# Attention 14 places earlier, output weights split under the gated unit, first down weights split when their pool opens

## The chip, the cores and the metric

The kernel runs on one core of one Trainium2 chip. The metric is the device time of one execution in microseconds (us); of several runs the median is given. TensorE is called PE in the profile, VectorE DVE, ScalarE ACT, GpSimd POOL and SyncE SP; PEld is TensorE's loading of weights.

## The reference

A layer norm of `x` (2048 tokens by 448), then two branches that are added to `x`: attention with a compressive memory, and a gated linear unit.

```python
xn = _layernorm(x)
# attention: 16 heads of 28, 4 segments of L = 512 tokens, one after the other
logits = einsum("bhqd,bhkd->bhqk", qs, ks) * scale + mask     # causal within the segment
a_dot = einsum("bhqk,bhkd->bhqd", softmax(logits), vs)
a_mem = (phi(qs) @ M) / (phi(qs) @ z + 1e-6)                  # phi(t) = t + 1 if t > 0 else exp(t)
o = g * a_mem + (1 - g) * a_dot                               # g = sigmoid(beta), per head
M, z = M + phi(ks).T @ vs, z + sum(phi(ks))
attn = concat(o) @ wo
# gated unit, F = 1792
glu = (sigmoid(xn @ w_gate) * (xn @ w_up)) @ w_down
out = x + attn + glu
```

## The kernel before

All products are done in float32r with operands split in two, a high part and the residue (`split`: ScalarE copies the high part, VectorE subtracts), and three products per pair of operands; a product over 448 is 11 matmuls of up to 512 columns (`TERMS`).

The program has three parts. The *front* (L236 to L471) normalises and transposes `x` block by block (4 blocks of 512 tokens), computes values (`values`, `pv`), keys and queries (`keys_queries`, `pp`), the memory (`update`) and its recall (`recall`, `n2`), and stores queries and keys (`qd`), values (`vd`) and recalled parts (`md`) to DRAM. Then *attention* and the *gated unit* run interleaved, and last `project` multiplies the attention's output (`od` in DRAM, loaded to `ob`, transposed in `transpose_split` to `xs`) by the output weights `wo` (`po`, L668) and adds it to `acc`, which already holds `x` and receives the gated unit's products (`pd`, L154, added at L157); the result is stored from `acc`.

The gated unit is a generator (`gated`): 7 pairs of 128-wide slices of F, for each pair 4 token blocks, for each block two gate and two up products (`pgu`, L209, 11 matmuls each) and up to four down products of earlier blocks (`down`, 6 matmuls each). Each `yield` is a place. A dictionary `ahead` says at which places the next weights are loaded and split: the raw gate and up weights pass through one buffer (`raw`), the split ones through three buffers of 8 KB (`8k`), the down weights through two raw buffers and four split ones (`wdn`) in the pool `late`, which is opened when the front's pool is closed. The first 18 places stand in the front already, between its last products; the first down weights (slices 0 and 1) are split by the entry `ahead[1, 1]`, L193, right after those 18 places.

Attention is another generator (`attention`), of 234 steps: 16 units of four heads, 14 steps each (`SLOT`). A unit is two pairs of heads. A pair loads its queries and keys (`Pair.load`, L490, six DMAs into one of two `qk2` buffers), makes scores (`st`, L506), copies them (L509), masks them on GpSimd (L518), finds maxima on VectorE (L521, L536 to L549), subtracts (L557) and exponentiates (L558). `Unit.finish` multiplies by the values (`pa`, L583), transposes (`n1`, L590), normalises to `on` (L125) and stores to `od` from GpSimd's queue (L596).

The main loop runs the gated unit's places and then the projection's; after each it runs as many attention steps as keep attention evenly spread over the places from `LEAD` to the end less `TAIL`:

```python
k = NG * FILL + 6                                   # 18
for part in (ffn, project()):
    for _ in part:
        want = min(round(n_att * (k - LEAD) / (N_FFN + N_OUT - LEAD - TAIL)), n_att)
```

`N_FFN` is 548 and `N_OUT` 77, so that 234 steps fall on 625 - 32 - 55 = 538 places, 0.435 steps to a place. `project` opens with the load of `ob` and then loads, through the one `raw` buffer, the two halves of the output weights, each split when it is in (L645 to L652). The six downs that are left when the gated unit ends (`rest`) are run in its first places. `po` takes its bank by turns from the tag of the down products (`pd`, one bank) and from the scores' (`s`).

TensorE's order is the order of the program (`MANUAL`), in the front that of ScalarE and VectorE too (`FRONT`). Everything else is ordered by a scheduler, queue by queue, and each engine and each DMA queue then works in that order: SP's queue holds nearly all loads and stores.

Of the kernel before, what the change touches and what calls it, by code (L numbers as in the profile page):

```python
# [16 lines left out]
P = 128  # L17
# [17 lines left out]

LEAD, TAIL = 32, 55

# [19 lines left out]
def kernel(  # L57
# [86 lines left out]

    rest, late = [], []

    def gated():
# [26 lines left out]
        def ready_down(f):  # L174
            wdn[f] = late[0].tile([P, 2, D], F32R, name="wdn", bufs=4)
            split(wdn[f][:, 0, :], wdn[f][:, 1, :], raw_down[f])

        load_up(0)
        yield
# [8 lines left out]
        for f0 in range(0, NF, FG):  # L188

            ahead = {}  # L190
            if f0 == 0:
                ahead[0, 0] = lambda: ready_up(1)
                ahead[1, 1] = lambda: (ready_down(0), ready_down(1))  # L193
            if f0 + FG < NF:
# [4 lines left out]
                ahead[3, 2] = lambda: ready_up(f0 + 3)  # L199
                ahead[3, 3] = lambda: ready_down(f0 + 3)  # L200
            for b in range(NB):
                hs = []
# [33 lines left out]
    with tc.tile_pool(name="front", bufs=2) as sb, tc.manual_schedule(engines=FRONT):  # L236
# [100 lines left out]
        def recall(b, i, phi):  # L337
# [4 lines left out]
            weigh(sb, tb, n2, gate[:, HG * i:HG * (i + 1)], MEM_EPS)  # L342
            nc.sync.dma_start(md[b][:, :, GW * i:GW * (i + 1)], tb.rearrange("p (t j) d -> p t (j d)", t=NT))

# [129 lines left out]

    late.append(ctx.enter_context(tc.tile_pool(name="late", bufs=1, reuse_waits="tile")))
    sb = ctx.enter_context(tc.tile_pool(name="att", bufs=1, reuse_waits="tile"))

# [159 lines left out]
    def project():  # L637
# [3 lines left out]
        def load(b):  # L641
            nc.sync.dma_start(ob[b % 2][:, :, :D].bitcast(F32), od[b])
            nc.sync.dma_start(ob[b % 2][:, :, D:].bitcast(F32), od[b][:, :, 384:])

        load(0)  # L645
        raw = [mid.tile([P, 1024], F32, name="raw", bufs=1)[:, :2 * D] for _ in range(2)]
        wo = [eight_k(F32R, f"wo{n}").rearrange("p c n -> p (c n)")[:, :4 * D] for n in range(2)]
        wo3 = w_o.rearrange("p (h n) -> p h n", h=2)
        for h in range(2):
            nc.sync.dma_start(raw[h], wo3[:, h, :])  # L650
            part = slice(2 * D * h, 2 * D * (h + 1))
            split(wo[0][:, part], wo[1][:, part], raw[h])  # L652
        load(1)
        yield
        for n in range(NB * NT + 3):
# [8 lines left out]
            if n >= 3:  # L664
                b, t = divmod(n - 3, NT)
                po = bank("po", ("pd", "s", "s")[n % 3])
                for m, (a, w) in enumerate(TERMS):
                    T.matmul(po[:, :D], xs[b][:, a, t * P:(t + 1) * P], wo[w // 4][:, D * (w % 4):D * (w % 4 + 1)],  # L668
                             start=m == 0, stop=m == len(TERMS) - 1)
                    if m in (3, 7):  # L670
                        yield
# [56 lines left out]
```

## Time and profile before

| | |
|---|---|
| median of 3 runs | 729.49 us (728.47 to 730.18) |
| profiled execution | 728.81 us, of which the span 727.1 us |
| granted TensorE clock | 0.99 of full speed over the span |
| gated unit's products (L209) | 1232 matmuls, mean 398 ns |
| down products (L154) | 672 matmuls, mean 373 ns |
| scores (L506), weighted values (L583) | 256 and 512 matmuls |
| projection (L668) | 176 matmuls |

The profile shows one execution. Matmuls are pipelined, so a mean of 398 ns is the time in the pipe, and a group of 11 takes 2.55 us. A timeline row has start, length (both us), engine, line, operation, the tiles out<-in, shapes, the count, and in brackets how long the engine stood idle before it and what ended that. A row of waits has the total, the count and the longest. A row of groups has the count, busy time, mean ns, and idle time before.

### The profile page before, as it was taken

How to read it: one execution, taken by the hardware profiler on the slowest of the kernel's cores; microseconds unless marked ns; L12 is line 12 of the kernel's file. 1: busy time of each engine (PE TensorE's matmuls, PEld its weight loads, DVE VectorE, ACT ScalarE, POOL GpSimd, SP SyncE). 2: the span in 40 equal slices, each digit the busy share in tenths (PEclk: the TensorE clock that was granted, in tenths of full speed). 3: DMA queues.
4: the chain of work that ended last, by engine and by line, in shares of the span. 5: the costliest groups of instructions: out<-in, count | busy, mean ns of one | idle time of the engine just before them, and what ended most of it. 6: DMA issues, size and time to landing. Idle time of an engine off the chain costs nothing.

```text
span 727.1 us, 10861 instructions
## 1 busy us (share of the span) xinstructions
PE 708.5 (97%) x3788; PEld 587.2 (81%) x3788; DVE 560.9 (77%) x1030; ACT 338.2 (47%) x552; POOL 147.9 (20%) x349
## 2 busy tenths in 40 slices
PE   7999999999999999999999999999999999998898
PEld 6888888887887877878878777787787877876697
DVE  5676776455599888898888898898788898888653
ACT  3635444231355554565545555455454555444320
POOL 4310000000131212222223223242222332322100
PEclk7999999999999999999999999999999999999999
DMA  9443546675343223322333225232422233223242
GB/s 311 185 174 133 218 178 236 227 252 134 98 106 86 74 66 94 107 78 67 109 103 88 59 83 133 71 88 79 127 66 73 64 92 85 82 74 110 84 159 89
DMA packets 58278, 86.24 MB, mean 119 GB/s; under 512 B 20080, under 2 KB 36976, under 8 KB 57712
## 3 DMA queue, kind: packets, MB, share of 16 engines
q1 hardware_dynamic: 56944, 81.88, 36.2%
q0 software_dynamic: 1280, 3.67, 1.4%
q8 instruction: 30, 0.49, 0.3%
q14 instruction: 24, 0.20, 0.1%
HBM read 53.81 MB, written 31.72 MB: 118 GB/s over the span
## 4 chain that ended last, share of the span: by engine, by line
PE 62%; DVE 18%; issue 8%; POOL 6%; ACT 3%; DMA 3%; SPq 0%; POOLq 0%; ACTq 0%; DVEq 0%
PE pgu L209 22%; PE pd L154 10%; PE pp L295 8%; PE pv L284 6%; PE po L668 5%; DVE mx L521 4%; DVE w L557 4%; PE st L506 3%; PE pa L583 3%; POOL w L518 2%; DVE acc L157 2%; DVE mb L549 2%; PE n L341 1%; PE pmm L323 1%; POOL on L595 1%
## 5 line engine op out<-in xcount | busy, mean ns | idle before, releaser
L209 PE MATMUL pgu<-xs,wgu 128*128 128x512 f32 x1232 | 321.7, 398 | 0.0
L209 PEld LDWEIGHTS pgu<-xs,wgu 128*128 128x128 f32 x1232 | 225.7, 188 | 44.9 <-issue 1.8
L154 PE MATMUL pd<-wdn,hh 128*128 128x448 f32 x672 | 165.3, 373 | 7.2 <-DVE acc L157 3.6
L154 PEld LDWEIGHTS pd<-wdn,hh 128*128 128x128 f32 x672 | 123.3, 190 | 23.7 <-DVE acc L157 3.7
L518 POOL TENSOR_SCALAR_AFFINE_SELECT w<-w 128x256 f32<-128x256 f32 (+1 forms) x160 | 72.1, 451 | 332.8 <-ACT w L509 330.9
L558 ACT ACTIVATE w<-w 128x1024 f32<-128x1024 f32 (+1 forms) x96 | 86.8, 914 | 84.3 <-DVE w L557 81.6
L521 DVE TRANSPOSE_TENSOR_REDUCE mx<-w 128x32 f32<-128x1024 f32 (+1 forms) x96 | 101.1, 1056 | 23.3 <-POOL w L518 23.1
L509 ACT ACTIVATE w<-st 128x512 f32<-128x512 f32 x160 | 93.5, 588 | 53.0 <-PE st L506 52.9
L557 DVE TENSOR_TENSOR w<-w,mb 128x1024 f32<-128x1024 f32 (+3 forms) x128 | 108.6, 872 | 0.4
L295 PE MATMUL pp<-xs,wqk 128*128 128x512 f32 x308 | 77.3, 399 | 0.0
L157 DVE TENSOR_TENSOR acc<-pd,acc 128x448 f32<-128x448 f32 x112 | 67.7, 606 | 8.0 <-PE pd L154 7.9
L295 PEld LDWEIGHTS pp<-xs,wqk 128*128 128x128 f32 x308 | 56.6, 189 | 11.8
L506 PE MATMUL st<-qk 84*128 84x128 f32 (+3 forms) x256 | 63.9, 311 | 0.0
L506 PEld LDWEIGHTS st<-qk 84*128 84x128 f32 x256 | 48.3, 189 | 8.9 <-ACT w L509 0.4
L220 ACT ACTIVATE hh<-sg 128x512 fp32r<-128x512 f32 x56 | 35.1, 626 | 43.5 <-DVE sg L218 38.4
L549 DVE STREAM_TRANSPOSE mb<-top 128x1024 f32<-128x1024 f32 x32 | 39.7, 1241 | 13.0 <-POOL top L546 12.9
L217 ACT ACTIVATE sg<-pgu 128x512 f32<-128x512 f32 x56 | 33.3, 595 | 34.7 <-PE pgu L209 34.5
L284 PE MATMUL pv<-wv,xs 128*128 128x448 f32 x176 | 42.2, 396 | 3.2 <-ACT xs L98 3.2
L221 DVE SCALAR_TENSOR_TENSOR hh<-sg,hh 128x512 fp32r<-128x512 f32 x56 | 39.6, 706 | 6.5 <-ACT hh L220 6.3
L218 DVE SCALAR_TENSOR_TENSOR sg<-sg,pgu 128x512 f32<-128x512 f32 x56 | 37.4, 668 | 9.0 <-PE pgu L209 8.8
L301 DVE TENSOR_TENSOR qk<-pp,qk 128x512 fp32r<-128x512 f32 x28 | 19.3, 690 | 30.7 <-ACT e L300 23.6
L284 PEld LDWEIGHTS pv<-wv,xs 128*128 128x128 f32 x176 | 35.0, 205 | 7.4 <-ACT xs L98 4.1
(94 smaller groups left out, 626.3 us busy)
## 6 DMA issues: line engine op xcount, KB each, us to landing
qk<-qd SPq DMA_DIRECT2D x192, 112.0 KB
qd<-qk SPq DMA_DIRECT2D x28, 512.0 KB
raw<-in_w_ffn SPq DMA_DIRECT2D x14, 512.0 KB
vd<-vst SPq DMA_DIRECT2D x4, 1024.0 KB
vv<-vd SPq DMA_DIRECT2D x16, 256.0 KB
od<-on POOLq DMA_DIRECT2D x16, 224.0 KB, 3.7
ob<-od SPq DMA_DIRECT2D x4, 896.0 KB
out<-acc SPq DMA_DIRECT2D x16, 224.0 KB
```

The source lines that it names most:

```text
L154: T.matmul(pd[:, :D], l, r, start=n == 0, stop=n == len(mms) - 1)
L157: V.tensor_add(acc[b][:, t, :], pd[:, :D], acc[b][:, t, :])
L209: T.matmul(dst, wgu[f][:, w, side * P:(side + 1) * P], xs[b][:, a, :], start=n == 0, stop=n == len(TERMS) - 1)
L284: T.matmul(pv[:, :D], xs[b][:, a, t * P:(t + 1) * P], wv[:, w, :], start=n == 0, stop=n == len(TERMS) - 1)
L295: T.matmul(pp, wqk[c][:, w, :], xs[b][:, a, :], start=n == 0, stop=n == len(TERMS) - 1)
L506: T.matmul(st[:, at:at + L - kb * P], self.qk[:KS, 1, h, kb * P:(kb + 1) * P], self.qk[:KS, 0, h, kb * P:], start=True, stop=True)
L509: A.activation(w, st, AF.Copy)
L518: G.affine_select(d, d, pattern=pattern, base=0, channel_multiplier=-1, compare_op=ALU.is_ge, fill=MASK)
L521: V.tensor_reduce(mx[:, 16 * n0:16 * (n + 1)], self.w[:, n0 * L:(n + 1) * L].rearrange("p (b n) -> p b n", n=32), axis=mybir.AxisListType. ...
L549: V.transpose(mb.rearrange("p h (b n) -> p (h b) n", n=32), top.rearrange("p h b -> p (h b)").unsqueeze(2).to_broadcast([P, 32, 32]))
L557: V.tensor_sub(w[:, :, a:b], w[:, :, a:b], mb[:, :, q0:])
L558: A.activation(w, w, AF.Exp, scale=SCALE)
```

## The change

Four edits:

- `LEAD, TAIL` go from 32, 55 to 18, 69. Their sum stays, so attention keeps its 0.435 steps to a place and starts and ends 14 places earlier.
- The output weights are loaded and split in the gated unit's last pair (`load_out`, `ready_out`), which has no next weights to prepare, into two of the 8 KB buffers, one for each half with its high and low part; `out_weights` finds a slice in them. The loads and splits in `project` go.
- The splits of the first two down weights go from the entry `ahead[1, 1]` to a call `begin[0]()` right behind the opening of `late`.
- The stores of recalled parts to `md` (12 in all, four for each of three blocks) are issued from GpSimd's queue and not from SP's.

Nothing is added to the matmuls and the vector work or taken from it.

```diff
--- before.py
+++ after.py
@@ -33,7 +33,7 @@
 MASK = -1e9 / SCALE
 FG = 2
 
-LEAD, TAIL = 32, 55
+LEAD, TAIL = 18, 69
 
 
 SLOT = (0, 0, 0, None, 0, 0, 2, 3, 1, 1, 1, None, 1, 1)
@@ -142,7 +142,7 @@
         return mid.tile([P, L], F32, name=name, tag="2k", bufs=2)
 
 
-    rest, late = [], []
+    rest, late, begin, wo = [], [], [], {}
 
     def gated():
 
@@ -175,6 +175,17 @@
             wdn[f] = late[0].tile([P, 2, D], F32R, name="wdn", bufs=4)
             split(wdn[f][:, 0, :], wdn[f][:, 1, :], raw_down[f])
 
+        raw_o = {}
+
+        def load_out(h):
+            raw_o[h] = mid.tile([P, 1024], F32, name="raw", bufs=1)[:, :2 * D]
+            nc.sync.dma_start(raw_o[h], w_o[:, 2 * D * h:2 * D * (h + 1)])
+
+        def ready_out(h):
+            wo[h] = eight_k(F32R, "wo").rearrange("p c n -> p (c n)")
+            split(wo[h][:, :2 * D], wo[h][:, 2 * D:4 * D], raw_o[h])
+
+        begin.append(lambda: (ready_down(0), ready_down(1)))
         load_up(0)
         yield
         ready_up(0)
@@ -190,7 +201,6 @@
             ahead = {}
             if f0 == 0:
                 ahead[0, 0] = lambda: ready_up(1)
-                ahead[1, 1] = lambda: (ready_down(0), ready_down(1))
             if f0 + FG < NF:
                 ahead[0, 2] = lambda: load_up(f0 + 2)
                 ahead[1, 2] = lambda: (ready_up(f0 + 2), load_down(f0 + 2))
@@ -198,6 +208,11 @@
                 ahead[2, 1] = lambda: (ready_down(f0 + 2), load_down(f0 + 3))
                 ahead[3, 2] = lambda: ready_up(f0 + 3)
                 ahead[3, 3] = lambda: ready_down(f0 + 3)
+            else:
+
+                ahead[0, 2] = lambda: load_out(0)
+                ahead[1, 2] = lambda: (ready_out(0), load_out(1))
+                ahead[3, 2] = lambda: ready_out(1)
             for b in range(NB):
                 hs = []
                 for f in range(f0, f0 + FG):
@@ -340,7 +355,7 @@
             for t in range(NT):
                 T.matmul(n2[:, t * P:(t + 1) * P], phi[:, t * P:(t + 1) * P], mst[b % 2][i], start=True, stop=True)
             weigh(sb, tb, n2, gate[:, HG * i:HG * (i + 1)], MEM_EPS)
-            nc.sync.dma_start(md[b][:, :, GW * i:GW * (i + 1)], tb.rearrange("p (t j) d -> p t (j d)", t=NT))
+            nc.gpsimd.dma_start(md[b][:, :, GW * i:GW * (i + 1)], tb.rearrange("p (t j) d -> p t (j d)", t=NT))
 
         raw = [four_k(F32, "wv_raw") for _ in range(2)]
         raw = [raw[t // 2][:, t % 2, :D] for t in range(4)]
@@ -473,6 +488,7 @@
 
 
     late.append(ctx.enter_context(tc.tile_pool(name="late", bufs=1, reuse_waits="tile")))
+    begin[0]()
     sb = ctx.enter_context(tc.tile_pool(name="att", bufs=1, reuse_waits="tile"))
 
     class Pair:
@@ -642,14 +658,11 @@
             nc.sync.dma_start(ob[b % 2][:, :, :D].bitcast(F32), od[b])
             nc.sync.dma_start(ob[b % 2][:, :, D:].bitcast(F32), od[b][:, :, 384:])
 
+        def out_weights(w):
+            at = 2 * D * (w // 4) + D * (w % 2)
+            return wo[w % 4 // 2][:, at:at + D]
+
         load(0)
-        raw = [mid.tile([P, 1024], F32, name="raw", bufs=1)[:, :2 * D] for _ in range(2)]
-        wo = [eight_k(F32R, f"wo{n}").rearrange("p c n -> p (c n)")[:, :4 * D] for n in range(2)]
-        wo3 = w_o.rearrange("p (h n) -> p h n", h=2)
-        for h in range(2):
-            nc.sync.dma_start(raw[h], wo3[:, h, :])
-            part = slice(2 * D * h, 2 * D * (h + 1))
-            split(wo[0][:, part], wo[1][:, part], raw[h])
         load(1)
         yield
         for n in range(NB * NT + 3):
@@ -665,7 +678,7 @@
                 b, t = divmod(n - 3, NT)
                 po = bank("po", ("pd", "s", "s")[n % 3])
                 for m, (a, w) in enumerate(TERMS):
-                    T.matmul(po[:, :D], xs[b][:, a, t * P:(t + 1) * P], wo[w // 4][:, D * (w % 4):D * (w % 4 + 1)],
+                    T.matmul(po[:, :D], xs[b][:, a, t * P:(t + 1) * P], out_weights(w),
                              start=m == 0, stop=m == len(TERMS) - 1)
                     if m in (3, 7):
                         yield
```

How the built programs' orders differ, at the two places that the prediction speaks of. Line numbers behind the diff are those of the changed kernel: L522 for L506, L224 for L209, L573 for L557, L599 for L583, L506 for L490.

TensorE where the front ends, before: `n` is the last recall, `pgu` the gated unit's products, `st` the first score product of the first pair.

```order
L341 MATMUL n_1661<-mst_3_126,phi 128x128 x4
L209 MATMUL pgu<-xs_68,wgu 128x512 x10
L154 MATMUL pd<-wdn,hh 128x448 x6
L209 MATMUL pgu<-xs_68,wgu 128x512 x11
L154 MATMUL pd<-wdn,hh 128x448 x6
L209 MATMUL pgu<-xs_69,wgu 128x512 x11
L154 MATMUL pd<-wdn,hh 128x448 x6
L209 MATMUL pgu<-xs_69,wgu 128x512 x8
L506 MATMUL st<-qk_1682 128x512
```

And now:

```order
L356 MATMUL n_1661<-mst_3_126,phi 128x128 x4
L224 MATMUL pgu<-xs_68,wgu 128x512 x10
L522 MATMUL st<-qk_1688 128x512
L154 MATMUL pd<-wdn,hh 128x448 x6
L522 MATMUL st<-qk_1688 128x384
L522 MATMUL st<-qk_1688 128x128
L224 MATMUL pgu<-xs_68,wgu 128x512 x8
L522 MATMUL st<-qk_1688 128x512
L224 MATMUL pgu<-xs_68,wgu 128x512 x3
L154 MATMUL pd<-wdn,hh 128x448 x6
```

The first score products stand right behind the products after the last recall, and the first of them ahead of the first down.

SP's queue at the same place, before: `raw` is a load of gate and up weights, `md` the last block's four stores, `qk` the loads of the first pairs.

```order
L164 DMA raw<-in_w_ffn 128x1024
L302 DMA qd_83<-qk 128x1024
L164 DMA raw<-in_w_ffn 128x1024
L343 DMA md_95<-tb 512x1x112 x4
L490 DMA qk_1682<-qd_80 28x2x512 x6
L490 DMA qk_1689<-qd_80 28x2x512 x6
L570 DMA vv<-vd_88 128x4x128
```

And now:

```order
L164 DMA raw<-in_w_ffn 128x1024
L317 DMA qd_83<-qk 128x1024
L164 DMA raw<-in_w_ffn 128x1024
L506 DMA qk_1688<-qd_80 28x2x512 x6
L506 DMA qk_1695<-qd_80 28x2x512 x6
L586 DMA vv<-vd_88 128x4x128
L168 DMA rawd<-in_w_ffn 128x448 x2
```

The four stores have left the queue (they stand on GpSimd's), and the pairs' loads follow the load of gate and up weights at once.

ScalarE at the same place, now; before, the rows up to the two splits are the same.

```order
L232 ACTIVATE sg<-pgu 128x512
L235 ACTIVATE hh<-sg 128x512
L232 ACTIVATE sg<-pgu 128x512
L82 ACTIVATE wdn<-rawd 128x448 x2
L525 ACTIVATE w<-st 128x512 x3
L235 ACTIVATE hh<-sg 128x512
```

The two splits of down weights stand behind the same `sg` as before; three score copies now stand ahead of the next `hh`.

VectorE where the projection begins, before: `mx`, `top`, `mb` and `w` are the softmax of the last pair, `wo` the second half's split, `xs` residues of the projection's transposes, `acc` the sums.

```order
L157 TENSOR_TENSOR acc_73<-pd,acc_73 128x448
L83 TENSOR_TENSOR wo_6811<-raw,wo_6810 128x896
L536 TENSOR_TENSOR mx<-mx 128x2x12
L157 TENSOR_TENSOR acc_73<-pd,acc_73 128x448
L537 TENSOR_TENSOR mx<-mx 128x2x4
L99 TENSOR_TENSOR xs_67<-pt,xs_67 128x3x128
L538 TENSOR_TENSOR mx<-mx 128x2x8
L100 TENSOR_TENSOR xs_67<-pt,xs_67 64x128
L542 TENSOR_TENSOR mx<-mx,up 64x2x16
L157 TENSOR_TENSOR acc_73<-pd,acc_73 128x448
L544 TENSOR_TENSOR top<-mx,up 32x32
L99 TENSOR_TENSOR xs_67<-pt,xs_67 128x3x128
```

And now the same stretch, from the last pair's `mb` to the first `xs`:

```order
L565 STREAM_TRANSPOSE mb<-top 128x1024
L573 TENSOR_TENSOR w<-w,mb 128x2x512
L157 TENSOR_TENSOR acc_73<-pd,acc_73 128x448
L573 TENSOR_TENSOR w<-w,mb 128x2x384
L573 TENSOR_TENSOR w<-w,mb 128x2x128
L573 TENSOR_TENSOR w<-w,mb 128x512
L233 SCALAR_TENSOR_TENSOR sg<-sg,pgu 128x512
L157 TENSOR_TENSOR acc_73<-pd,acc_73 128x448
L236 SCALAR_TENSOR_TENSOR hh<-sg,hh 128x512
L157 TENSOR_TENSOR acc_73<-pd,acc_73 128x448
L99 TENSOR_TENSOR xs_67<-pt,xs_67 128x3x128
L100 TENSOR_TENSOR xs_67<-pt,xs_67 64x128
```

The last softmax and the split stood among the first `xs`; now the softmax ends ahead of the last `sg` of the gated unit, and no split is left there.

TensorE there, before, from the last scores (`st`) to the first `po`; `pt` are the projection's transposes:

```order
L154 MATMUL pd<-wdn,hh 128x448 x3
L506 MATMUL st<-qk_6321 128x256 x2
L154 MATMUL pd<-wdn,hh 128x448 x9
L94 MATMUL pt<-ident_r,ob 128x128 x4
L154 MATMUL pd<-wdn,hh 128x448 x6
L94 MATMUL pt<-ident_r,ob 128x128 x4
L154 MATMUL pd<-wdn,hh 128x448 x6
L94 MATMUL pt<-ident_r,ob 128x128 x4
L154 MATMUL pd<-wdn,hh 128x448 x6
L94 MATMUL pt<-ident_r,ob 128x128 x4
L668 MATMUL po<-wo_6810,xs_67 128x448
```

And now, from the last gated product on; a transpose, a down and a transpose follow behind these rows, then the first `po`:

```order
L224 MATMUL pgu<-xs_70,wgu 128x512 x11
L154 MATMUL pd<-wdn,hh 128x448 x12
L94 MATMUL pt<-ident_r,ob 128x128 x4
L154 MATMUL pd<-wdn,hh 128x448 x6
L599 MATMUL pa<-w,vv 32x512 x4
L599 MATMUL pa<-w,vv 32x384 x4
L599 MATMUL pa<-w,vv 32x256 x4
L599 MATMUL pa<-w,vv 32x128 x4
L94 MATMUL pt<-ident_r,ob 128x128 x4
L154 MATMUL pd<-wdn,hh 128x448 x3
L606 MATMUL n_6896<-ident,w 128x128 x4
L154 MATMUL pd<-wdn,hh 128x448 x3
```

The last unit's `pa` and `n` stood behind the first `po` and now stand among the first transposes.

## The prediction

> **What bounds the kernel now.** I read the page first, then the busy time by stretches, then what TensorE waited for, then the order of time around each place where it stood still.
>
> ```profile
> PE 708.5 (97%) x3788; PEld 587.2 (81%) x3788; DVE 560.9 (77%) x1030; ACT 338.2 (47%) x552; POOL 147.9 (20%) x349
> ```
>
> ```profile
> 158.00:200.00 42.00, 40.60 (x197) 33.84 (x196) 22.15 (x42) 13.32 (x23) 1.84 (x5) 1.00 0.44 126
> 400.00:450.00 50.00, 49.12 (x273) 39.09 (x273) 45.26 (x74) 27.73 (x42) 14.22 (x31) 1.00 0.33 89
> ...
> 650.00:680.00 30.00, 23.05 (x112) 19.47 (x111) 26.18 (x44) 12.57 (x19) 4.91 (x11) 0.94 0.34 103
> 680.00:727.00 47.00, 43.53 (x261) 38.10 (x261) 21.81 (x44) 7.77 (x13) 1.88 (x2) 0.99 0.31 106
> ```
>
> The columns are length, busy PE, PEld, DVE, ACT, POOL, then the granted clock. TensorE executes in order and is the bound: between 40 and 650 us it idles 1.40 us in one stretch (42.00 - 40.60) and 0.88 us in another. The change alters no matmul, so it can only win idle time, and that lies in 650 to 680: 30.00 - 23.05 = 6.95 us, at a clock of 0.94, with DVE busy for 26.18 of 30. These are TensorE's waits:
>
> ```profile
> PE pd L154 <- DVE acc L157: 3.6, 1, 3.6
> ...
> PE pd L154 <- DVE acc L672: 2.3, 1, 2.3
> ...
> PE pd L154 <- ACT wdn L82: 1.2, 1, 1.2
> PE po L668 <- DVE acc L157: 1.1, 1, 1.1
> ```
>
> 3.6, 2.3 and 1.1 make up the 6.95 us; the 1.2 belongs to 158 to 200. In order of time:
>
> ```profile
> 663.75 0.95 ACT L82 ACTIVATE wo<-raw 128x896 fp32r<-128x896 f32 x1 [2.88 <-DMA raw<-in_w_o]
> 664.61 0.61 ACT L220 ACTIVATE hh<-sg 128x512 fp32r<-128x512 f32 x1
> ...
> 665.26 0.69 DVE L221 SCALAR_TENSOR_TENSOR hh<-sg,hh 128x512 fp32r<-128x512 f32 x1 [1.95 <-ACT hh L220]
> ...
> 667.39 1.07 DVE L83 TENSOR_TENSOR wo<-raw,wo 128x896 fp32r<-128x896 f32 x1
> 667.52 2.12 PE L154 MATMUL pd<-wdn,hh 128*128 128x448 f32 x6 [3.57 <-DVE acc L157]
> ...
> 669.90 2.21 PE L154 MATMUL pd<-wdn,hh 128*128 128x448 f32 x6
> ...
> 673.52 0.46 PE L94 MATMUL pt<-ident_r,ob 128*128 128x128 f32 x4
> ...
> 675.11 2.51 PE L668 MATMUL po<-wo,xs 128*128 128x448 f32 x11 [1.13 <-DVE acc L157]
> ...
> 677.76 0.62 DVE L157 TENSOR_TENSOR acc<-pd,acc 128x448 f32<-128x448 f32 x1
> 678.31 0.55 DVE L99 TENSOR_TENSOR xs<-pt,xs 128x384 fp32r<-128x384 f32 x1
> 678.87 0.29 DVE L100 TENSOR_TENSOR xs<-pt,xs 64x128 fp32r<-64x128 f32 x1
> 679.19 0.62 DVE L672 TENSOR_TENSOR acc<-po,acc 128x448 f32<-128x448 f32 x1
> 679.87 1.49 PE L154 MATMUL pd<-wdn,hh 128*128 128x448 f32 x6 [2.25 <-DVE acc L672]
> ```
>
> ScalarE stands behind the second load of output weights for 2.88 us; the `hh` copy behind it is late, DVE idles 1.95 us for that copy, the bank of the down product is freed late, and TensorE waits 3.57 us. The two groups of six after it take 2.12 and 2.21 us where the group at 679.87 takes 1.49: that slower clock costs (2.12 - 1.49) + (2.21 - 1.49) = 1.35 us. DVE never catches up, because the last pair's softmax lies in the same place, and the later waits of 1.13 and 2.25 us follow. Together 6.95 + 1.35 = 8.3 us.
>
> **The change part by part.** (1) *Attention 14 places earlier, output weights split under the gated unit.* Per pair DVE spends on its softmax:
>
> ```profile
> L521 DVE TRANSPOSE_TENSOR_REDUCE mx<-w 128x32 f32<-128x1024 f32 (+1 forms) x96 | 101.1, 1056 | 23.3 <-POOL w L518 23.1
> L557 DVE TENSOR_TENSOR w<-w,mb 128x1024 f32<-128x1024 f32 (+3 forms) x128 | 108.6, 872 | 0.4
> L549 DVE STREAM_TRANSPOSE mb<-top 128x1024 f32<-128x1024 f32 x32 | 39.7, 1241 | 13.0 <-POOL top L546 12.9
> ```
>
> (101.1 + 108.6 + 39.7) / 32 = 7.8 us. The order shows these rows of the last pair move from among the first transposes of the projection to ahead of the last `sg`, and the last `pa` and `n` move in among those transposes. The stretch from the last gated downs to the first `po` then holds less for DVE and more for TensorE:
>
> ```profile
> 682.52 2.29 PE pa L583 x32
> ...
> 686.87 1.22 PE pd L154 x6
> ...
> 693.64 2.32 PE po L668 x11
> ```
>
> ```profile
> 653.96 0.62 DVE L125 TENSOR_TENSOR on<-n,rc 128x448 f32<-128x448 f32 x1
> ```
>
> From the down ahead of the first transpose to the last transpose before `po`, TensorE has 4 downs of 1.22, 4 transposes of 0.46, `pa` 2.29 and `n` about as long as a transpose: 9.5 us. DVE has 4 additions of 0.62, 4 residues of 0.55 + 0.29, and the `on` step, 0.62 and a few tenths of small steps (0.4 taken): 6.9 us. So DVE keeps up there, where before it also had most of the 7.8 us and a 1.07 us split. No wait for a load is left: the second output load stands many rows ahead of its split, and the split waits only for the last product that reads the gate weights whose buffer it takes; the `hh` copy behind it on ScalarE is not read before the sixth down from there.
>
> What stays late: the `pd` bank taken by the first `po` is asked for again by the next down, so TensorE waits for the addition at L672 as at 679.87. Ahead of that addition DVE then has, counted from the end of `pa`: two ScalarE copies of 0.6 (as at 664.61), xs 0.84, `on` 1.0, two additions 1.24, two xs 1.68 = 6.0 us, and TensorE has 2 x 1.22 + 3 x 0.46 + 0.46 + 2.32 = 6.6 us. DVE is just in time, and the wait is the addition itself, 0.62 us, and its semaphores: 1.0 us. One more wait of about 0.4 us is likely at the fourth down of the projection, whose bank is freed right behind the last softmax. Residue 1.4 us, bounds 0 and 4.2 (half of what is lost now). These waits are shorter than the 2.25 us after which the clock was unharmed, so the 1.35 us go too. Gain 8.3 - 1.4 = 6.9 us.
>
> The two splits themselves are hidden: they cost ScalarE and DVE about 1 us each at a place where DVE is busy for at most 45.26 of 50 and TensorE is the bound. Without that cover each would cost up to 1.07 us.
>
> (2) *Start of attention, md stores on POOL's queue.*
>
> ```profile
> 155.13 2.71 PE L295 MATMUL pp<-xs,wqk 128*128 128x512 f32 x11
> ...
> 164.42 11.40 SPq L343 DMA_DIRECT2D md<-tb  x4
> ...
> 175.17 0.60 ACT L217 ACTIVATE sg<-pgu 128x512 f32<-128x512 f32 x1 [1.86 <-PE pgu L209]
> 175.67 1.03 ACT L82 ACTIVATE wdn<-rawd 128x448 fp32r<-128x448 f32 x2
> 175.92 5.33 SPq L490 DMA_DIRECT2D qk<-qd  x12
> ...
> 176.29 0.47 PE L154 MATMUL pd<-wdn,hh 128*128 128x448 f32 x1 [1.21 <-ACT wdn L82]
> ...
> 187.47 0.40 PE L506 MATMUL st<-qk 84*128 84x512 f32 x1
> ```
>
> The first score product stood at 187.47; now it is the row ahead of the first down, which TensorE reaches at 176.29 - 1.21 = 175.08. Its six loads used to queue on SP behind four md stores that wait for DVE, 164.42 to 175.8. With those gone SP comes to them at about 164.4; the front's tiles under them were last read by the matmuls that end at 157.84. Six issues take 5.33 / 2 = 2.67 us and landing this long:
>
> ```profile
> 391.85 2.35 DMA qk<-qd
> ```
>
> That makes 169.4, 5.7 us ahead of need. On POOL's queue nothing stands behind these stores but copies of `xn` that come later in DVE's order anyway, and nobody reads md before the second block's units.
>
> (3) *First down weights.* ScalarE's order is the same as before here: the `sg` at 175.17 first, then the two splits at 175.67. TensorE still waits, less the score product that now fills some of it: gain 0.2 us, bounds 0 and 1.4.
>
> (4) In the middle I expect the same small stalls in other places: net 0, from -0.9 (the 0.88 us gone) to +3.
>
> **Sum.** The profiled execution took 728.81 us, of which 727.1 is the span. 728.81 - 6.9 - 0.2 = 721.7. It lay 0.68 us below the median of the runs (729.49), so for the median I say 722.4 us.
>
> **The rivals.** *Transition only half cured* (0.12): DVE is as late as today after `pa`, residue 4.2: 725.2. For it speaks DVE's 26.18 of 30; against it that its work there falls by more than 7 us.
>
> *Pair loads late* (0.07): moving the stores saves SP only the time of their issue.
>
> ```profile
> 136.01 0.51 SPq L343 DMA_DIRECT2D md<-tb  x1
> ```
>
> Four of 0.51 are 2.0 us, loads begin at 173.9, land at 178.9, and TensorE waits 3.8 us, which covers the wait in (3), so 2.6 more: 725.0. Against it: the 11.40 us row is SP waiting, not issuing. The Trainium skill states this rule ("Trainium Kernel Development and Optimization", Key Constraints): issuing from several engines "only saves the sequencer's issue time". The row differs, since a queue in order also holds what stands behind a waiting store.
>
> *The stall only moves* (0.11): the load of the first output half is issued late, at the start of the last gated pair, and ScalarE and DVE both stand at its split as at 663.75; TensorE loses 3.57 + 1.35 = 4.9 us there: 727.3, more than half of such cases within 0.2% of before. Against it: that split is surrounded by gated matmuls, whose banks are double.
>
> *Slower* (0.06): with all phases shifted, ScalarE is caught behind raw weight loads more often, ahead of the copy that the `n` transposes need:
>
> ```profile
> 437.78 1.06 ACT L82 ACTIVATE wgu<-raw 128x1024 fp32r<-128x1024 f32 x1 [0.49 <-DMA raw<-in_w_ffn]
> ...
> 439.38 0.66 PE L590 MATMUL n<-ident,w 128*128 128x128 f32 x4 [0.88 <-ACT w L586]
> ```
>
> TensorE loses this once in the whole trace, with 14 such loads, at 0.88 us. It decides from 8 more hits (7.1 / 0.88); 11 more give 722.4 + 9.7 = 732.1. Against it: gated places and attention keep their ratio.
>
> **How the numbers follow.** The forecast has 0.64, at 722.4. Low end: residue 0 (-1.4), all of (3) (-1.2), no stall in the middle (-0.9): 718.9. High end: past both 725s and most of the 727.3 case: 727.3. 0.2% is 1.5 us, about what a measurement can tell here. Faster by more: 0.64 + 0.12 + 0.07 + 0.04 = 0.87; within: 0.07; slower: 0.06.
>
> **What would show it.** Right: no TensorE wait over 1.5 us where the projection begins, clock 1.00 there, pair loads issued from about 164, first score at about 175, a down at about 176.3 still behind ScalarE's splits. Wrong: TensorE waiting for a load at about 175, ScalarE behind `raw<-in_w_o` with TensorE idle, or more waits of TensorE between 200 and 640 than the 0.88 us above.

## The result and the profile after

The changed kernel takes 722.83 us, the median of 4 runs (721.91 to 723.76); the kernel before took 729.29 us beside it (4 runs, 728.47 to 730.18). The ratio is 0.992, with a 95% interval from 0.9907 to 0.9934: 6.46 us less. The forecast was 722.4 us. The profiled execution of the changed kernel took 723.55 us with a span of 721.9 us.

TensorE's busy time by stretches, after (length, busy PE, PEld, DVE, ACT, POOL, granted clock):

```profile
158.00:200.00 42.00, 40.84 (x201) 34.18 (x200) 29.41 (x55) 17.01 (x30) 8.12 (x17) 1.00 0.47 128
...
400.00:450.00 50.00, 49.43 (x254) 40.71 (x253) 43.59 (x70) 26.01 (x41) 15.08 (x33) 1.00 0.34 96
...
500.00:550.00 50.00, 47.94 (x262) 38.22 (x261) 42.02 (x73) 25.56 (x40) 12.52 (x33) 0.97 0.35 90
550.00:600.00 50.00, 49.25 (x252) 40.31 (x251) 41.90 (x68) 25.32 (x40) 12.83 (x33) 1.00 0.34 85
600.00:650.00 50.00, 49.25 (x271) 38.73 (x270) 42.94 (x71) 24.68 (x39) 13.92 (x34) 1.00 0.26 73
650.00:680.00 30.00, 29.28 (x172) 24.16 (x171) 23.40 (x43) 11.04 (x17) 4.46 (x9) 1.00 0.29 92
```

Where the projection begins, 650 to 680, TensorE idles 0.72 us instead of 6.95, at a clock of 1.00 instead of 0.94. In the middle it now idles more. One stretch of the kernel before belongs beside this, with 0.40 us of idle time that the prediction's reading left out:

```profile
500.00:550.00 50.00, 49.60 (x253) 40.79 (x252) 42.71 (x72) 26.17 (x42) 14.51 (x34) 1.00 0.31 87
```

Between 200 and 650 us the idle time is (50.00 - 49.43) + (50.00 - 47.94) + 2 x (50.00 - 49.25) = 4.13 us, where before it was the 0.88 us of 400 to 450, which the prediction shows, and these 0.40, 1.28 in all. So 6.23 us were won at the projection's start and 2.85 us lost again on the way there.

The projection's start in order of time, after:

```profile
656.37 0.96 ACT L82 ACTIVATE wo<-raw 128x896 fp32r<-128x896 f32 x1 [1.96 <-PE pgu L224]
...
662.69 1.89 DVE L573 TENSOR_TENSOR w<-w,mb 128x768 f32<-128x768 f32 x3
...
666.46 1.45 PE L154 MATMUL pd<-wdn,hh 128*128 128x448 f32 x6
...
677.32 1.49 PE L154 MATMUL pd<-wdn,hh 128*128 128x448 f32 x6 [0.72 <-DVE acc L685]
```

The second split waits for the last product that reads the gate weights, not for its load; DVE's last softmax steps end at 664.6, ahead of the first transposes; the down that waited 3.57 us for DVE now starts at once, and its six products take 1.45 us instead of 2.12. One wait is left, 0.72 us, on the bank of the first output product.

The start of attention, after:

```profile
161.42 7.32 SPq L506 DMA_DIRECT2D qk<-qd  x12
...
172.52 0.40 PE L522 MATMUL st<-qk 84*128 84x512 f32 x1
...
173.89 0.47 PE L154 MATMUL pd<-wdn,hh 128*128 128x448 f32 x1 [0.97 <-ACT wdn L82]
```

The pair loads start at 161.42 instead of 175.92, and the first score waits for nothing. In the middle, the largest new stall:

```profile
510.44 1.22 DVE L83 TENSOR_TENSOR wgu<-raw,wgu 128x1024 fp32r<-128x1024 f32 x1
...
511.71 0.36 SPq L164 DMA_DIRECT2D raw<-in_w_ffn  x1
...
516.84 1.06 ACT L82 ACTIVATE wgu<-raw 128x1024 fp32r<-128x1024 f32 x1 [1.80 <-DMA raw<-in_w_ffn]
517.80 0.58 ACT L602 ACTIVATE w<-pa 128x512 f32<-128x512 f32 x1
...
518.43 0.66 PE L606 MATMUL n<-ident,w 128*128 128x128 f32 x4 [2.06 <-ACT w L602]
...
518.85 1.99 PE L154 MATMUL pd<-wdn,hh 128*128 128x448 f32 x6
```

The only buffer for raw weights is free when DVE's half of the split before it is done, at 511.66. The load is issued then and is there at 516.8. ScalarE stands at its split, the copy of the attention product stands behind the split, and TensorE behind the copy.

### The profile page after: what moved, and what is told of

It reads as the page before. It is cut to its first block, busy times and chain, and to the rows that moved or that the text cites. A ratio compares the mean times of both kernels' runs of the same rounds, so it can differ in the third digit from the quotient of the medians.

```text
span 721.9 us, 10864 instructions
## 1 busy us (share of the span) xinstructions
PE 706.7 (98%) x3788; PEld 584.0 (81%) x3788; DVE 561.2 (78%) x1030; ACT 337.7 (47%) x552; POOL 155.0 (21%) x361
## 4 chain that ended last, share of the span: by engine, by line
PE 54%; DVE 23%; issue 10%; POOL 6%; ACT 3%; DMA 2%; SPq 1%; POOLq 0%; ACTq 0%; DVEq 0%
PE pgu L224 17%; PE pd L154 9%; PE pp L310 8%; DVE mx L537 5%; PE po L681 5%; PE pv L299 4%; DVE w L573 4%; DVE mb L565 3%; POOL w L534 3%; DVE acc L157 2%; PE st L522 2%; PE pa L599 2%; POOL on L611 2%; PE n L356 2%; PE pmm L338 1%
## 5 line engine op out<-in xcount | busy, mean ns | idle before, releaser
L224 PE MATMUL pgu<-xs,wgu 128*128 128x512 f32 x1232 | 322.5, 399 | 0.0
L224 PEld LDWEIGHTS pgu<-xs,wgu 128*128 128x128 f32 x1232 | 226.6, 189 | 45.1 <-issue 1.8
L573 DVE TENSOR_TENSOR w<-w,mb 128x1024 f32<-128x1024 f32 (+3 forms) x128 | 108.3, 869 | 0.4
L522 PE MATMUL st<-qk 84*128 84x128 f32 (+3 forms) x256 | 64.5, 313 | 2.1 <-ACT w L525 2.1
L522 PEld LDWEIGHTS st<-qk 84*128 84x128 f32 x256 | 48.5, 189 | 11.9 <-ACT w L525 3.6
L565 DVE STREAM_TRANSPOSE mb<-top 128x1024 f32<-128x1024 f32 x32 | 39.8, 1243 | 15.2 <-POOL top L562 15.1
L299 PE MATMUL pv<-wv,xs 128*128 128x448 f32 x176 | 39.0, 372 | 2.5 <-ACT xs L98 2.0
L311 ACT ACTIVATE qk<-pp 128x512 fp32r<-128x512 f32 x28 | 16.7, 597 | 50.8 <-PE pp L310 36.6
```

The lines of the kernel that those rows point to most:

```text
L224: T.matmul(dst, wgu[f][:, w, side * P:(side + 1) * P], xs[b][:, a, :], start=n == 0, stop=n == len(TERMS) - 1)
L299: T.matmul(pv[:, :D], xs[b][:, a, t * P:(t + 1) * P], wv[:, w, :], start=n == 0, stop=n == len(TERMS) - 1)
L522: T.matmul(st[:, at:at + L - kb * P], self.qk[:KS, 1, h, kb * P:(kb + 1) * P], self.qk[:KS, 0, h, kb * P:], start=True, stop=True)
L565: V.transpose(mb.rearrange("p h (b n) -> p (h b) n", n=32), top.rearrange("p h b -> p (h b)").unsqueeze(2).to_broadcast([P, 32, 32]))
L573: V.tensor_sub(w[:, :, a:b], w[:, :, a:b], mb[:, :, q0:])
```

## The experiments

Times are medians of 4 to 12 runs, each beside the kernel before on the same chip, which had 728.96, 728.73 and 727.88 us on the three chips. Where kernels from two chips are compared, the ratios to the kernel before are given.

**The memory stores' queue.** The first edit puts the stores back on SP:

```diff
-            nc.gpsimd.dma_start(md[b][:, :, GW * i:GW * (i + 1)], ...)
+            nc.sync.dma_start(md[b][:, :, GW * i:GW * (i + 1)], ...)
```

> The changed kernel with the memory stores back on SP's queue; the rows of TensorE, ScalarE and DVE stay in the same order. Theory (SP stands behind a store until DVE has made its tile, and the pair loads behind it stand too, as in the 11.40 us row of the kernel before): the pair loads start at about 172 instead of 161.4, land at about 176 to 177, and TensorE, whose first score stands at 172.5, waits 3 to 5 us for them, of which the 0.97 us wait for ScalarE behind it is covered: 725 to 727. Rival (a store on another queue only saves the time of its issue, 4 of about 0.5 us): the loads start at about 163.5, land before 172.5, and the time stays within 0.7 us of the changed kernel's, 722 to 723.5.

It took 729.82 us; the ratio is 1.0013 (1.0002 to 1.0023). The whole gain is gone. SP's queue and the first score, in this kernel:

```profile
162.00 11.41 SPq L358 DMA_DIRECT2D md<-tb  x4
...
173.52 5.52 SPq L506 DMA_DIRECT2D qk<-qd  x12
...
179.81 0.79 PE L522 MATMUL st<-qk 84*128 84x512 f32 x1 [7.14 <-DMA qk<-qd]
...
180.41 2.44 PE L154 MATMUL pd<-wdn,hh 128*128 128x448 f32 x6
```

The mechanism is the expected one and its price is larger: 6.3 us from the first issue to the score, 7.14 us of waiting, and the six products behind it at 2.44 us instead of 1.45. The Trainium skill's rule ("Trainium Kernel Development and Optimization", Key Constraints) that issuing from several engines only saves the time of issue does not cover this: what was saved is the standing of an in-order queue behind stores that were not ready.

The shift alone, in the kernel before:

```diff
-LEAD, TAIL = 32, 55
+LEAD, TAIL = 18, 69
```

> The kernel before with attention 14 places earlier and nothing else (LEAD, TAIL = 18, 69). Theory (the pair loads behind the four memory stores on SP's queue cost about what the shift wins): the first score waits about 7 us for its loads at 173, the projection's start loses 1 to 2 us instead of 8.3: 728.5 to 731. Rival (the parts add up, the shift is worth the whole 6.4 us by itself): 722 to 724.

729.82 us, ratio 1.002 (1.0006 to 1.0033). The parts don't add up: without the stores' move the shift is slightly slower than no shift. The wait was as long as expected:

```profile
PE st L506 <- DMA qk<-qd: 6.6, 1, 6.6
```

Half the shift with the stores on SP:

```diff
-LEAD, TAIL = 18, 69
+LEAD, TAIL = 25, 62
...
-            nc.gpsimd.dma_start(md[b]...
+            nc.sync.dma_start(md[b]...
```

> Half the shift with the memory stores back on SP's queue. Its first score stands at 179.2 us instead of 172.5. Theory (SP comes to the pair loads at about 173 and the first six land 6.3 us later, at about 179.5, whatever the shift): TensorE waits 0.2 to 1 us for them instead of 7: 719.2 to 720.5, so that the memory stores' move is needed for the full shift only. Rival (stores on SP cost the whole 7 us in any order, through what is queued behind them): 725 to 727.

719.90 us, ratio 0.988 (0.9864 to 0.9897). Here SP comes to the pair loads as late as with the full shift:

```profile
174.34 5.33 SPq L506 DMA_DIRECT2D qk<-qd  x12
...
180.54 0.50 PE L522 MATMUL st<-qk 84*128 84x512 f32 x1
```

The loads are issued as late, but the first score now stands behind their landing, and no wait is left, less than the 0.2 to 1 us expected. The same kernel with the stores on POOL's queue, further below, has 0.9872, which cannot be told from it. So it is the full shift that needs the stores' move.

**The projection's start.** The shift undone:

```diff
-LEAD, TAIL = 18, 69
+LEAD, TAIL = 32, 55
```

> The changed kernel with attention back at its old place (LEAD, TAIL = 32, 55); the output weights' split stays in the last gated pair, the memory stores on POOL's queue. Theory (both parts are needed: the split sets off the first wait of 3.57 us and the slow clock of 1.35 us, the last pair's softmax on DVE the later waits of 1.13 and 2.25 us): the first goes, the later ones stay, so TensorE's lost time between the last gated products and the first output products is 3 to 4 us and the time is 725 to 727. Rival A (the shift alone counts, DVE's softmax of 7.8 us is the whole cause): 727.5 to 729.5, with waits adding to 6 us or more. Rival B (the split alone counts, ScalarE standing behind the second output load): 722 to 724, and the profile shows waits under 1.5 us in all there.

725.57 us, ratio 0.9956 (0.994 to 0.9973). The waits there:

```profile
663.92 1.48 PE L154 MATMUL pd<-wdn,hh 128*128 128x448 f32 x6 [1.14 <-DVE acc L157]
...
670.52 2.51 PE L681 MATMUL po<-wo,xs 128*128 128x448 f32 x11 [1.66 <-DVE acc L157]
...
675.29 1.95 PE L154 MATMUL pd<-wdn,hh 128*128 128x448 f32 x6 [2.26 <-DVE acc L685]
```

5.06 us of the 6.95 stay, more than the 3 to 4 expected: the 3.57 us shrink to 1.14, and the two later waits, which fall where the last softmax stands among DVE's rows, stay whole. The time fell by 3.4 us all the same, more than the 6.95 - 5.06 = 1.9 us that are won here. The granted clock goes the same way, 0.996 in the mean of this kernel's runs against 0.992 for the kernel before.

The output weights' split put back at the start of the projection, with the shift:

```diff
-            else:
-                ahead[0, 2] = lambda: load_out(0)
-                ahead[1, 2] = lambda: (ready_out(0), load_out(1))
-                ahead[3, 2] = lambda: ready_out(1)
...
         load(0)
+        raw = [mid.tile([P, 1024], F32, name="raw", bufs=1)[:, :2 * D] for _ in range(2)]
+        ...
+        for h in range(2):
+            nc.sync.dma_start(raw[h], wo3[:, h, :])
+            part = slice(2 * D * h, 2 * D * (h + 1))
+            split(wo[0][:, part], wo[1][:, part], raw[h])
         load(1)
```

> The changed kernel with the output weights loaded and split at the start of the projection as before; attention stays 14 places earlier. Theory (both parts needed): the second split again stands on ScalarE and DVE ahead of the last hh copy, so the first down behind a transpose waits for DVE; with the softmax out of the way DVE catches up behind it, so 1.5 to 4 us are lost: 724 to 727. Rival A (the shift alone counts): 722 to 723.7, no wait beyond the 0.72 us of the changed kernel. Rival B (the split alone counts): 727.5 to 729.5, TensorE's first wait 3 us or more at a slower clock.

722.85 us, ratio 0.9924 (0.9908 to 0.994). My theory that both parts are needed falls; rival A holds by the time, though not to the letter. The split does stand there again:

```profile
663.33 1.08 DVE L83 TENSOR_TENSOR wo<-raw,wo 128x896 fp32r<-128x896 f32 x1
...
665.72 1.49 PE L154 MATMUL pd<-wdn,hh 128*128 128x448 f32 x6 [1.01 <-DVE acc L157]
```

It costs 1.01 us, and in the profile about as much is given back in the middle, where the stall at about 516 is 1.70 us instead of 2.06 and the six products behind it take 1.47 us instead of 1.99. With attention's end out of the way, the place of the split hardly counts.

Half the shift, all else as in the changed kernel (LEAD, TAIL = 25, 62):

> The changed kernel with half the shift (LEAD, TAIL = 25, 62). On DVE the last pair's softmax then ends between the first and the second transposes' residues, not between those and the output products. Theory (what counts is that the 7.8 us of softmax lie ahead of the transposes): most of the gain is there, one wait of about 1 us behind the first transposes and the 0.7 us behind the first output product stay: 723 to 725. Rival (each place of the shift is worth the same): half way between the unshifted 725.6 and the full 722.8, with a wait at the first output product of half its 1.7 us: also about 724, told apart by the waits; if no wait over 0.8 us is left, the theory undercounts the free time and half the shift is enough: 721.5 to 723.

719.12 us, ratio 0.9872 (0.9849 to 0.9895): better than the full shift, and outside what any theory gave. The waits at the projection's start are near the expected ones, 1.12, 0.38 and 1.13 us; it is the middle that differs:

```profile
200.00:650.00 450.00, 449.65 (x2434) 365.18 (x2433) 391.23 (x653) 240.13 (x377) 120.26 (x297) 1.00 0.32 87
```

TensorE idles 0.35 us there, against 4.13 with the full shift.

The bank of the first output product, and of every third after it:

```diff
-                po = bank("po", ("pd", "s", "s")[n % 3])
+                po = bank("po", ("s", "s", "s")[n % 3])
```

> The changed kernel with the first output product, and every third after it, in a bank of the scores instead of the bank of the downs. Theory (the one wait left where the projection begins, 0.72 us of a down behind the addition of the first output product, is a wait for that bank): it goes and nothing is late next, as the two score banks are free there: 0.5 to 1 us less, 721.8 to 722.4, and no wait of TensorE over 0.3 us between 660 and the end. Rival (DVE as a whole is late there, the bank only shows it): the next output product waits instead, for its bank or for xs, and the time stays within 0.3 us or rises.

721.49 us, ratio 0.9896 (0.988 to 0.9912), which overlaps the 0.9907 to 0.9934 of the changed kernel, so the times alone don't part them. The profile does: the 0.72 us are gone and nothing is late next.

```profile
650.00:690.00 40.00, 40.00 (x234) 34.19 (x232) 29.14 (x54) 12.84 (x20) 5.11 (x11) 1.00 0.29 89
```

The same bank with half the shift:

> Half the shift with the other bank for the first output product, one raw buffer. Theory: of the half shift's three waits at the projection's start (1.1, 0.4 and 1.1 us) the last, behind the addition of the first output product, is the bank's and goes: 717.5 to 718.8. Rival (DVE is late there, the bank only shows it): 718.8 to 720.

718.41 us, ratio 0.9863 (0.9848 to 0.9877). Again the wait behind the output product, 1.13 us, is gone and the two ahead of it stay (1.07 and 0.39 us); the time cannot be told from that of half the shift alone.

The third part of the change does nothing by itself: with the first down weights' split back at its old place, every engine of the changed kernel gets the same rows with the same waits in the same order. The 0.24 us by which the wait there fell are the first score's, which now fills a part of it.

**The middle.** Two kernels, both with the other bank. The control keeps the attention output and the memory tile inside the pair's finished weights; the other uses that room for a second raw buffer:

```diff
-            on = sb.tile([P, NT * HG, DH], F32, name="on")
+            on = self.pairs[1].w[:, L:L + D].rearrange("p (m d) -> p m d", d=DH)
...
-                self.tb = sb.tile([P, NT, GW], F32, name="tb")
+                self.tb = self.pairs[1].w[:, 2 * L:2 * L + D].rearrange("p (t d) -> p t d", t=NT)
...
-            raw_up[f] = mid.tile([P, 1024], F32, name="raw", bufs=1)
+            raw_up[f] = mid.tile([P, 1024], F32, name="raw", bufs=2)
```

(The last pair of lines, and the same for the output weights, is in the second kernel only; both have `up` in one buffer.)

> Control for the kernel with two raw buffers: the same tiles kept inside the pair's finished weights, but still one raw buffer. Theory: 721.0 to 722.2 as without it, the stalls at about 440, 516 and 594 us still there. Rival (the memory tile's load now waits until the product that reads the weights is done, and what comes behind it on SP with it): slower by 1 us or more, with TensorE waiting for loads.

> The kernel with the bank of the first output product changed (721.5 us), and two buffers instead of one for the raw gate, up and output weights; room for it is made by keeping the attention output and the memory tile inside the pair's finished weights. Theory (the stalls that the changed kernel gained in the middle, at 440, 516 and 594 us with 0.57, 2.06 and 0.75 us, are all ScalarE standing at a split whose raw load was issued late, because the one raw buffer is freed only by DVE's half of the split before): these 3.4 us go, and the slow clock behind the one at 516 (about 1.5 us) with them: 716.5 to 718.5, and no wait of TensorE for ScalarE's n copy is left. Rival (the order is the cause: a split of 1.06 us on ScalarE ahead of that copy stalls TensorE even with its data there): 0.6 to 1 us stays at each place, 719 to 721.5.

The control took 718.99 us (0.9868, 0.9846 to 0.989), the kernel with two raw buffers 716.26 us (0.9826, 0.9804 to 0.9848), on the same chip and with no run of the one in the range of the other. The second is the fastest of the study. What ScalarE waits for at raw loads, and TensorE for ScalarE, between 200 and 650 us; with one buffer and the two tiles in their old places:

```profile
ACT wgu L82 <- DMA raw<-in_w_ffn: 6.3, 3, 3.9
ACT wo L82 <- DMA raw<-in_w_o: 2.3, 1, 2.3
PE st L522 <- ACT w L525: 2.1, 3, 0.8
PE n L606 <- ACT w L602: 2.0, 1, 2.0
```

The control:

```profile
ACT wgu L82 <- DMA raw<-in_w_ffn: 4.8, 3, 2.9
ACT wo L82 <- DMA raw<-in_w_o: 2.1, 1, 2.1
PE st L522 <- ACT w L525: 1.5, 3, 0.7
```

Two raw buffers:

```profile
PE st L522 <- ACT w L525: 0.2, 1, 0.2
```

With two buffers ScalarE waits for no raw load at all, and TensorE's idle time falls to 0.28 us (450.00 - 449.72). The rival is answered by the control, in which the split still stands right ahead of the copy for the `n` transposes:

```profile
514.59 1.06 ACT L82 ACTIVATE wgu<-raw 128x1024 fp32r<-128x1024 f32 x1 [1.18 <-DMA raw<-in_w_ffn]
...
516.18 0.66 PE L606 MATMUL n<-ident,w 128*128 128x128 f32 x4
```

Even 1.18 us late it holds nothing up, so there the place of the split alone does not stall TensorE. With two buffers the split stands at 509.88 and not right ahead of that copy, so that kernel does not test the rival at this place; elsewhere in it a split with its data there, behind an exponential, costs TensorE 0.21 us (at 582.17).

The control was not neutral: moving two tiles changed the order on DVE and ScalarE enough that the stall at 516 was gone without a second buffer. By the ratios (0.9896, 0.9868, 0.9826) that is about 2 of the 5 us between the first kernel of the three and the last, with intervals of the first two that just overlap. The second buffer changes ScalarE's and DVE's order once more, while TensorE's stays. So the 2.7 us between the last two belong to the buffer together with the order that comes with it.

Then two tests of the phase. Half the shift with two raw buffers and the other bank:

> Half the shift (LEAD, TAIL = 25, 62) together with two raw buffers and the other bank for the first output product. Theory (half the shift is faster than the full one, 719.1 against 722.8, only because its phase meets no late raw load in the middle; two raw buffers take those away for any phase): nothing is left for the phase to win, and half the shift brings back its waits of 1.1 and 0.4 us behind the first transposes: 716.5 to 718.5, no better than the full shift with two raw buffers, 716.3. Rival (half the shift is better by itself): 713 to 715.5.

717.44 us, ratio 0.9853 (0.9837 to 0.9869). With two buffers half the shift is no longer better than the full one (0.9826), which fits the theory: its lead came from the middle. And attention begun 7 places later but ended at the same place, one raw buffer, the other bank (LEAD, TAIL = 25, 69):

> Attention begins 7 places later than in the changed kernel and ends at the same place (LEAD, TAIL = 25, 69), the first output product in the other bank, one raw buffer: the end of the full shift with another phase in the middle. Theory (the projection's start is set by where attention ends, the middle by the phase at which a raw load is asked for): no wait over 0.4 us from 655 on, as in the full shift with that bank; the waits for ScalarE in the middle are others than the 0.57, 2.06 and 0.75 us, between 0 and 4 us in all: 717 to 722. Rival (the middle's stalls come with the earlier end): 721 to 722.5, with about the same three waits.

724.15 us, ratio 0.9944 (0.9931 to 0.9958), above the expected range. The place is as the theory has it: between 650 and 690 TensorE is busy for all 40.00 us. The middle is worse than I allowed, 5.26 us idle:

```profile
200.00:650.00 450.00, 444.74 (x2398) 358.42 (x2397) 387.82 (x650) 237.16 (x373) 118.79 (x294) 1.00 0.31 86
```

Three kinds of wait make up most of it. The first is known, a late raw load (2.45 us in two waits, of which the longer is the first pair of rows). At the second ScalarE stands behind its own exponentials (1.40 us in three waits, the second pair). At the third, 1.04 us at 613.51, the copy for the `n` transposes stands behind an `hh` copy that is waiting for DVE:

```profile
594.35 0.95 ACT L82 ACTIVATE wo<-raw 128x896 fp32r<-128x896 f32 x1 [4.72 <-DMA raw<-in_w_o]
...
596.36 0.50 PE L522 MATMUL st<-qk 84*128 84x512 f32 x1 [1.51 <-ACT w L525]
```

```profile
467.60 1.05 ACT L574 ACTIVATE w<-w 128x1024 f32<-128x1024 f32 x1
468.54 0.59 ACT L525 ACTIVATE w<-st 128x512 f32<-128x512 f32 x1
...
469.18 0.50 PE L522 MATMUL st<-qk 84*128 84x512 f32 x1 [0.97 <-ACT w L525]
```

So raw loads explain about half of the loss here. The second kind was in the changed kernel too (0.75 us at about 647), where raw loads explain 0.57 + 2.06 + 0.75 of the 4.13 us. With two buffers that wait is gone as well; whether the buffers or the new order did that, no run shows.

## Why the prediction was right

The time and the sign came out as forecast, by the likeliest case, though one step of the sum failed. Step by step:

*The transition.* Right, and a little better than its size: 8.3 - 0.72 = 7.6 us won where 6.9 stood. The wait behind the first output product was 0.72 us instead of 1.0, for the reason given (the bank; taking another bank removes it), and the 0.4 us at the fourth down did not appear. What the step had wrong is how the gain divides: I read the stall as set off by the output weights' split, and it was mainly what the shift takes away. With the shift, the split's old place costs 1.01 us; without the shift, 5.06 us stay. That DVE's last softmax is what counts in it, the unshifted kernel's profile shows: from 663.88 to 675.23 DVE waits for nothing, and 4.45 us of that softmax (L565 and L573) stand between the additions that TensorE waits for. No run moves it alone.

*The stores' queue.* Right in direction and landing: the loads begin at 161.42, the first score stands at 172.52, with its loads there. The rival that prices their late arrival at 3.8 us, 725.0 in all, was mis-sized: with the stores on SP the wait is 7.14 us and the time 729.82. The sum took the landing from single loads, 2.35 us, and let the first score stand at 175.08; with all twelve in one queue and a score at 172.67 both terms were too kind.

*The first down weights.* Right: 1.40 - 1.16 = 0.24 us less idle between 158 and 200, and the down at 173.89 still stands behind ScalarE's splits.

*The middle.* This step failed. "Net 0, from -0.9 to +3" was 2.85 us of idle time, and the six products at 518.85 took 1.99 us where such a group takes 1.45, with the clock of its stretch at 0.97. The clock of that stretch stands for (1 - 0.97) x 50 = 1.5 us, so about 4.3 us were lost, beyond the upper end. The mechanism was named, as the case in which ScalarE is caught behind raw loads, but its price of 0.88 us a hit came from the one hit in the trace of before, and the hits depend on the phase: 1.28 us of idle time before, 4.13 in the changed kernel, 0.35 with half the shift, 5.26 with another pace (2.45 of it behind raw loads). Two of the signs that the prediction names for being wrong are there as well: more waits between 200 and 640 than the 0.88 us, and ScalarE behind `raw<-in_w_o` with TensorE idle. The second belongs to the rival that the stall only moves to the first output half's split, which came in at a small size:

```profile
592.20 0.95 ACT L82 ACTIVATE wo<-raw 128x896 fp32r<-128x896 f32 x1 [2.29 <-DMA raw<-in_w_o]
...
594.21 0.50 PE L522 MATMUL st<-qk 84*128 84x512 f32 x1 [0.75 <-ACT w L525]
```

*The sum.* With the terms as measured it is -7.6 - 0.24 + 4.3 = -3.5 us, and the medians differ by 6.46. The rest is not in the places that I priced; the clock outside them accounts for it in size. In the profile of before, the first 40 us had it:

```profile
0.00:40.00 40.00, 34.60 (x149) 29.07 (x150) 27.05 (x71) 19.35 (x39) 15.43 (x22) 0.87 0.69 251
```

In the profile of after, the same work:

```profile
0.00:40.00 40.00, 34.66 (x168) 28.35 (x169) 29.59 (x75) 20.77 (x41) 15.67 (x23) 1.00 0.69 257
...
152.75 2.71 PE L310 MATMUL pp<-xs,wqk 128*128 128x512 f32 x11
```

The eleven products at 152.75 stood at 155.13 before: 2.38 us, before anything that the change touches in TensorE's order. With them the two profiles nearly close: -3.5 - 2.38 = -5.9 us, where the profiled executions differ by 728.81 - 723.55 = 5.26. But the late start is not a need of the kernel before. In the profiles of the other twelve kernels these products stand at 152.47 to 153.51, with the shift alone, which has the same order on TensorE up to there, at 153.25, and the clock of their first 40 us is 0.96 or 1.00. The unshifted kernel, whose time fell by more than its waits explain, has them at 152.86.

The mean granted clock of the kernel before was 0.992 over 17 runs on one chip (0.988 to 0.997), that of the changed kernel 0.997 over its 4 runs (0.994 to 1.000); 0.005 of 725 us is 3.6 us. So the clock is of the missing size. How much of it belongs to the longer waits of the kernel before and how much to a start that varies from run to run stays open, since only one profile of that kernel exists. The sign and the two ends of the shift came out for the reasons given. That the time came within half a microsecond is luck: a middle that cost more and a clock that gave more nearly cancel.

## What to carry to other kernels

Before work is moved earlier, look at what stands in its loads' queue: here four stores that waited for their data made the full shift worthless, and a queue of their own made it pay. A gain read at one end of a shift is only half of the account; a shift changes the phase of everything between, and a single load buffer whose release hangs on a late instruction turns some phases into stalls, which a second buffer took away at both phases that were tried. A control that only makes room for the experiment is needed: here the scheduler made another order of it, and it was worth about 2 us by itself.

## What the runs showed of the hardware

The granted clock falls after shorter waits than I took: in the changed kernel it is 0.59 from 519 to 522 us, behind the wait of 2.06 us. After a wait of 1.70 us in the kernel with the old split (first pair of rows) six products took 1.47 us; after 2.02 us at the same place in the kernel with the other bank (second pair) they took 2.24, and the clock from 519 to 522 us is 1.00 in the one and 0.63 in the other:

```profile
518.60 0.66 PE L601 MATMUL n<-ident,w 128*128 128x128 f32 x4 [1.70 <-ACT w L597]
519.01 1.47 PE L154 MATMUL pd<-wdn,hh 128*128 128x448 f32 x6
```

```profile
518.99 0.66 PE L606 MATMUL n<-ident,w 128*128 128x128 f32 x4 [2.02 <-ACT w L602]
519.40 2.24 PE L154 MATMUL pd<-wdn,hh 128*128 128x448 f32 x6
```

Of the waits between 2.0 and 2.3 us some are followed by a slow group (2.02, 2.06, 2.26) and some not (2.25 in the kernel before, 2.14 in the unshifted one). The Trainium skill ("TensorE: Matmul & The Clock Gate", Part 1) has the clock halve after an idle window of about 3.4 us, in windows that run freely. That it differs from case to case agrees with free-running windows; that 2.02 us can be enough does not agree with a whole idle window, and the measurement decides.

Stores on POOL's queue can land later than DVE wants its tile back: in the changed kernel they land 2.6 to 6.9 us after their issue. In the kernel before, with the stores on SP, DVE never waited for `md<-tb`. In the changed kernel it waited 0.51 and 0.61 us, without effect on TensorE, and in the kernel with two raw buffers 1.83 us, where TensorE stood idle for 0.70 us, up to 170.00, ahead of the `n` products behind it. Why they land late, no run shows:

```profile
169.27 0.63 DVE L125 TENSOR_TENSOR tb<-n,rc 128x448 f32<-128x448 f32 x1 [1.83 <-DMA md<-tb]
```
